# A first MLP layer by seven products in halves of 128 tokens, with its weight factors streamed from device memory

## The chip, the cores and the metric

The kernel runs on one core of one Trainium2 chip. The metric is the device time of one execution in microseconds (us), taken several times; the median counts. Beside the times there is one profiled execution, and all durations below come from it. Engines are named as the profile names them: PE multiplies matrices and PEld loads its stationary operand, DVE and ACT and POOL work on vectors (PSUM, where PE leaves its sums, is read by DVE and ACT alone), and SP is a queue that issues transfers and does nothing else here.

## The reference

Attention with a threshold, and then a two-layer MLP over the same tokens:

```python
q, k, v: (8, 8, 576, 64) float32         # batch, heads, sequence, head dim
scores = (1 / sqrt(64)) * q @ k^T
scores = where(scores >= max(scores) - tau, scores, -1e9)
attn   = softmax(scores) @ v
x      = attn as (8 * 576, 512)           # 4608 tokens, heads side by side
h      = x @ w_in                         # w_in: (512, 2048)
g      = max(h, 0) ** 2
out    = g @ w_out                        # w_out: (2048, 512)
```

Everything is float32. A float32 matmul stands in the profile as two records, each with a weight load of its own.

## The kernel before

All engines run in an order written out by the program: the order in which the Python code issues instructions is the order of each engine's queue, and each queue is strictly in order.

**Attention.** Two heads are a pair; there are 32 pairs (8 batches of 4). A visit goes through the 576 queries of one pair in steps of 128 queries. Loop `for s in range(END + 1)` (L851) takes one step: `scores` (PE, L246, into the two PSUM tiles `s0`, `s1`, then a maximum by DVE, L268), `exponents` (ACT, L281 to L284), `threshold` (DVE, L296), `divide` (POOL, L304 and L306), all on the same step. In the larger part of the run (steps from `first_dma` on) the step's weights are transposed one step later in blocks of 32x32 by DVE (`turn_blocks`, L370, into `turned`), and `place_blocks` moves the blocks into the tile `wT` by transfers of 36 or 72 KB that SP issues (L382, L387), 16 for each two steps. There is one `wT`. At the end of a visit `mix` (PE, L432) multiplies `wT` with the values and ACT copies the result to `xT`, a ring of 5 x 256 tokens.

**MLP.** The 4608 tokens are 18 chunks of 256. When a batch's attention is done, its chunks join the list `waiting` as pieces of about 1.76 us of PE time (`PIECE_US`). `fill` (L769) takes pieces from this list four times a step, so that PE has work while the other engines do attention. A piece returns a function with the work on its result (reading PSUM out, squaring); `after` (L760) issues this function behind the next piece's matmuls, and what that function returns behind the one after.

Chunk 0 is plain in both layers. In chunks 1 to 15 the first layer is plain (`mlp_in`, L473: 16 pieces of 4 matmuls, 128x128 weights against 256 tokens, two pieces to a PSUM bank, then relu on ACT, L492, and the square on POOL, L493). Their second layer is `product` (L540): the seven products of Strassen's scheme in Winograd's form, each 8 matmuls of 128 tokens' sums against 256 columns. `square_half` (POOL, L470, L471) makes two of the sums that it needs. The last two chunks, 16 and 17, share one first layer by seven products in halves of 256 tokens (`pair_in`, L635): its operands' sums are made by DVE (`pair_sums`), `w_in` stays in SBUF, and the seven results are put together by DVE (L659 to L668).

`next_bank` (L315) hands out PSUM banks 4 to 7 in turn; `mix`, `mlp_in` and `product` all take from it.

Of the kernel before, what the change touches and what calls it, by code (L numbers as in the profile page):

```python
# [9 lines left out]
FP32 = mybir.dt.float32  # L10
U32 = mybir.dt.uint32
AF = mybir.ActivationFunctionType
ALU = mybir.AluOpType
# [6 lines left out]
def kernel(  # L20
# [24 lines left out]
    HF, HD = NFT // 2, d_model // 2  # L45
    SCALE = 0.125
# [5 lines left out]
    psum = ctx.enter_context(tc.tile_pool(name="psum", bufs=1, space=bass.MemoryType.PSUM))  # L52

# [4 lines left out]


# [34 lines left out]
    p1s = const.tile([P, HD], FP32, name="p1s")  # L94
    p5s = const.tile([P, HD], FP32, name="p5s")
# [213 lines left out]
    used = {"tx": 0, "mm": 0, "bank": 7}  # L309

# [4 lines left out]
    def next_bank():  # L315

        among = (4, 5, 6, 7) if state["step"] > first_dma + 2 else (6, 7)
        used["bank"] = min([x for x in among if x > used["bank"]] or among)
        return bank[used["bank"]]

# [146 lines left out]
    def square_half(lo, g=g, gsum=gsum):  # L467

        f = slice(lo, lo + HF // 2)
        nc.gpsimd.tensor_tensor(out=gsum[0][:, f, :], in0=g[:, f, P:], in1=g[:, lo + HF:lo + HF + HF // 2, P:], op=ALU.add)  # L470
        nc.gpsimd.tensor_tensor(out=gsum[1][:, f, :], in0=gsum[0][:, f, :], in1=g[:, f, 0:P], op=ALU.subtract)  # L471

    def mlp_in(j, x):  # L473

        f, at = FORDER[x], j * TCH % RING
        if x % 2 == 0:
            used["h"] = take("mm", (6, 7)) if j < PLAIN else next_bank()
# [6 lines left out]
        posts = []  # L484
        if j == PAIR - 1 and x > 1:
            posts.append(lambda: pair_sums(1, PAIR_EARLY))
        if j == PLAIN:
            posts.append(lambda: some_sums(1))
        if x % 2:
            def square():  # L490
                to = g[:, f - 1:f + 1, :]
                nc.scalar.activation(out=to, in_=h, func=AF.Relu)  # L492
                nc.gpsimd.tensor_tensor(out=to, in0=to, in1=to, op=ALU.mult)  # L493
                if j >= PLAIN and x % 8 == 7:
                    square_half(x // 8 * (HF // 2))
            posts.append(square)
        return posts
# [40 lines left out]
    PRODUCTS = ("1", "5", "6", "2", "7", "4", "3")  # L538

    def product(j, x, half):  # L540

        if half == 0:
            used["p"] = next_bank()
        to = used["p"][:, 0:HD]
        p = PRODUCTS[x]
        g, gsum = (g_pair, gsum_pair) if j == PAIR + 1 else squares
# [9 lines left out]
        if j == PAIR - 1:  # L556
            pair_sums(1, 0)
# [7 lines left out]
        def then():  # L565
            add, sub, tt, u = ALU.add, ALU.subtract, nc.vector.tensor_tensor, u_sum
            if p == "1":
# [25 lines left out]
    squares = g, gsum  # L593
    PAIR = NCH - 2
    at0, at1, at2 = (x * TCH % RING for x in (PAIR, PAIR + 1, PAIR + 2))
    assert (at1, at2) == (at0 + TCH, at0 + 2 * TCH) and at2 + 2 * TCH <= RING
    DH = d_ff // 2
    wT_flat = wT.rearrange("p c n -> p (c n)")
    mS1, mS2 = (wT_flat[:, x * 2 * DH:(x + 1) * 2 * DH].rearrange("p (c n) -> p c n", c=2) for x in range(2))
    g_pair = turned[:, 0:NFT * TCH].rearrange("p (f n) -> p f n", f=NFT)  # L600
    flat_slots = [x.rearrange("p u k -> p (u k)") for x in w_slots[0:2]]
    gsum_pair = [x[:, 0:HF * P].rearrange("p (f n) -> p f n", f=HF) for x in flat_slots]
    xS = [flat_slots[x // 2][:, x % 2 * 2 * TCH:(x % 2 + 1) * 2 * TCH].rearrange("p (c n) -> p c n", c=2)
          for x in range(4)]
    x11, x12, x21, x22 = (xT[:, c:c + 2, at:at + TCH] for c in (0, 2) for at in (at0, at1))
    temps = [x[:, 0:2 * TCH] for x in (qT, kT[0], kT[1])] + [wT_flat[:, 4 * DH:4 * DH + 6 * TCH]]
    temps = [x[:, i:i + TCH] for x in temps for i in range(0, x.shape[1], TCH)]
    pair_p1, pair_tmp = temps[0:2], temps[2:]

    def quarter_sums():  # L610

        add, sub = ALU.add, ALU.subtract
        cols = [(c, slice(h * WP, (h + 1) * WP), slice(DH + h * WP, DH + (h + 1) * WP)) for c in range(2) for h in range(2)]
        for c, lo, hi in cols:
            yield mS1[:, c, lo], w_in_sb[:, c, hi], w_in_sb[:, 2 + c, hi], add
        for c, lo, hi in cols:
            yield mS2[:, c, lo], mS1[:, c, lo], w_in_sb[:, c, lo], sub
        yield xS[0], x12, x11, sub
        yield xS[1], x22, xS[0], sub
        yield xS[2], x22, x12, sub  # L620
        yield xS[3], xS[1], x21, sub
        for c, lo, hi in cols:
            yield w_in_sb[:, c, hi], w_in_sb[:, c, lo], w_in_sb[:, c, hi], sub
        for c, lo, hi in cols:
            yield xT[:, 2 * c + lo.start // WP, at2:at2 + WP], w_in_sb[:, 2 + c, lo], mS2[:, c, lo], sub

    quarters = list(quarter_sums())
    PAIR_EARLY = 8

    def pair_sums(count, keep):  # L630
        for to, a, b, op in quarters[:max(min(count, len(quarters) - keep), 0)]:
            nc.vector.tensor_tensor(out=to, in0=a, in1=b, op=op)
            quarters.pop(0)

    def pair_in(j, f):  # L635

        assert not quarters
        lo, hi = slice(f * P, (f + 1) * P), slice(DH + f * P, DH + (f + 1) * P)
        S4 = [xT[:, 2 * c + f // 4, at2 + f % 4 * P:at2 + f % 4 * P + P] for c in range(2)]
        part = {1: ([w_in_sb[:, c, lo] for c in range(2)], x11), 2: ([w_in_sb[:, 2 + c, lo] for c in range(2)], x21),  # L640
                3: (S4, x22), 4: ([w_in_sb[:, 2 + c, hi] for c in range(2)], xS[3]),
                5: ([mS1[:, c, lo] for c in range(2)], xS[0]), 6: ([mS2[:, c, lo] for c in range(2)], xS[1]),
                7: ([w_in_sb[:, c, hi] for c in range(2)], xS[2])}
        if f == 0:
            used["pair"] = [psum.tile([P, 2, 512], FP32, tag=f"s{u}", name=f"pair{u}")[:, 0, :] for u in range(2)]
            used["pair"] += [bank[x] for x in range(4, 8)]
        ps = {}
        for x, what in enumerate(((1, 6), (2, 7), (5, 3), (4,))):
            b = used["pair"][(4 * f + x) % 6].rearrange("p (h n) -> p h n", h=2)
            for y, p in enumerate(what):  # L650
                ps[p] = b[:, y, :]
                for c in range(2):
                    nc.tensor.matmul(ps[p], part[p][0][c], part[p][1][:, c, :], start=(c == 0), stop=(c == 1))  # L653

        def then():
            add, sub, tt = ALU.add, ALU.subtract, nc.vector.tensor_tensor
            p1 = pair_p1[f % 2]
            nc.scalar.copy(p1, ps[1])
            u2, u3, u4, c11, c12, c21, c22 = pair_tmp[0:7]  # L659
            tt(out=u2, in0=ps[6], in1=p1, op=add)  # L660
            tt(out=c11, in0=ps[2], in1=p1, op=add)
            tt(out=u3, in0=ps[7], in1=u2, op=add)
            tt(out=u4, in0=ps[5], in1=u2, op=add)
            tt(out=c22, in0=ps[5], in1=u3, op=add)
            tt(out=c12, in0=ps[3], in1=u4, op=add)
            tt(out=c21, in0=u3, in1=ps[4], op=sub)
            for to, c in ((g[:, f, :], c11), (g[:, HF + f, :], c21), (g_pair[:, f, :], c12), (g_pair[:, HF + f, :], c22)):
                nc.vector.scalar_tensor_tensor(out=to, in0=c, scalar=0.0, in1=c, op0=ALU.max, op1=ALU.mult)  # L668
            if f % 4 == 3:
                square_half(f - 3)  # L670
            if f == HF - 1:
                for x in (0, HF // 2):
                    square_half(x, g_pair, gsum_pair)
        return [then]

# [13 lines left out]
    PLAIN = 1  # L691
# [38 lines left out]
    def pieces_of(j):  # L730

        todo = [((x // 4 + 1) * NMC, mlp_in, j, x) for x in range(NFT)]
        if j >= PAIR:
            todo = [(n_pieces, pair_in, j, f) for f in range(HF)] if j == PAIR else []
        if j < PLAIN:
            todo += [(n_in + min(f + 1 + f // (NFT - 2), NFT), mlp_out, j, f) for f in range(NFT)]
        else:
            todo += [(n_pieces, product, j, x, half) for x in range(len(PRODUCTS)) for half in range(2)]
        return todo

    def add_chunk(j):
        waiting.extend(pieces_of(j))

# [25 lines left out]
    def fill(us):  # L769
        state["left"] += us  # L770
        while waiting and state["left"] >= PIECE_US / 2 and waiting[0][0] <= state["usable"]:
            _, fn, *what = waiting.popleft()
            state["left"] -= PIECE_US
            if fn in (mlp_out, pair_in) or what[0] in (*range(PLAIN + 1), PAIR) and what[1] == 0:
                after()
# [18 lines left out]
    def end_rounding(p):  # L794
        round_weights(p, 4)
        state["rounded"] += 1
        if p + RAW < n_pieces:
            load_weights(p + RAW)
# [182 lines left out]
```

## Time and profile before

| | |
|---|---|
| median of 3 runs | 1380.3 us (1380.26 to 1381.9) |
| the profiled execution's span | 1377.9 us, 2.4 us under the median |
| PE busy | 1345.0 us, 98% of the span |
| DVE, ACT, POOL busy | 874.8, 433.3, 880.8 us |
| first layer, chunks 0 to 15 (L480) | 2048 matmul records |
| first layer, chunks 16 and 17 (L653) | 224 matmul records |
| SP: transfers into `wT` (L382, L387) | 992 |
| POOL: transfers of q, k, v (L190) | 416 |

A record's duration runs from its start to the last result written, and the next record starts before that; so spacing between starts, not duration, is what a record costs PE. The table of engines therefore does not tell how close PE is to its limit; the chain of waits and the timeline do.

### The profile page before, as it was taken

The numbers are of one execution on the slowest core, as the hardware profiler recorded it, in microseconds if no ns is written. First come the engines' busy times: TensorE is split into PE (matmuls) and PEld (weight loads), VectorE is DVE, ScalarE is ACT, GpSimd is POOL, SyncE is SP. The second block draws the span as 40 slices with busy tenths as digits, with TensorE's granted clock in tenths as the row PEclk, the third lists the DMA queues.
The fourth block names the chain that finished last, engine by engine and source line by source line (L and its number), as shares of the span: only waits on it lengthen the run. The fifth ranks groups of instructions, "written<-read, shape, count | busy, mean of one in ns | idle before, by whom it ended". The sixth has DMA issues, their size and how long they took to land.

```text
span 1377.9 us, 22712 instructions
## 1 busy us (share of the span) xinstructions
PE 1345.0 (98%) x7544; PEld 1031.9 (75%) x7544; DVE 874.8 (63%) x1974; ACT 433.3 (31%) x1060; POOL 880.8 (64%) x1193
## 2 busy tenths in 40 slices
PE   6898999999999999999999999999999999999998
PEld 5676557777777777777777777777777777788887
DVE  6877675967767676757575666566666666432551
ACT  4777674223232323232322222222222232200000
POOL 3678874768786868676767768585868665513121
PEclk8999999999999999999999999999999999999999
DMA  8764530445646455554445455545445544320000
GB/s 154 161 153 112 148 87 25 91 84 106 118 95 116 98 107 118 103 114 86 96 84 114 87 112 107 105 74 105 89 104 98 118 82 94 64 56 0 16 0 31
DMA packets 407875, 127.94 MB, mean 93 GB/s; under 512 B 390832, under 2 KB 396752, under 8 KB 407760
## 3 DMA queue, kind: packets, MB, share of 16 engines
q1 hardware_dynamic: 385632, 95.10, 36.6%
q0 software_dynamic: 19824, 31.11, 8.4%
q8 instruction: 61, 1.00, 0.3%
q10 hardware_dynamic: 2304, 0.29, 0.2%
q14 instruction: 54, 0.44, 0.1%
HBM read 50.59 MB, written 9.44 MB: 44 GB/s over the span
## 4 chain that ended last, share of the span: by engine, by line
PE 89%; ACT 3%; DVE 3%; POOL 2%; issue 1%; DMA 1%; SPq 0%; ACTq 0%; DVEq 0%; POOLq 0%
PE bank L480 31%; PE bank L555 29%; PE s L246 12%; PE bank L432 11%; PE bank L653 2%; PE bank L521 2%; PE bank L330 2%; PE pair L653 1%; ACT wT L331 1%; ACT w L284 1%; DVE wo L509 1%; DVE w L296 1%; DVE st L268 1%; POOL g L493 0%; POOL w L306 0%
## 5 line engine op out<-in xcount | busy, mean ns | idle before, releaser
L480 PE MATMUL bank<-xT,w_in_sb 128*128 128x256 f32 x2048 | 464.8, 383 | 3.1 <-POOL w_in_sb L147 2.1
L480 PEld LDWEIGHTS bank<-xT,w_in_sb 128*128 128x128 f32 x2048 | 382.1, 190 | 79.2 <-issue 21.7
L268 DVE TENSOR_REDUCE st<-s 128x1 f32<-128x576 f32 x286 | 204.1, 752 | 220.8 <-PE s L246 220.8
L296 DVE SCALAR_TENSOR_TENSOR w<-s,st,w 128x576 f32<-128x576 f32 x269 | 209.3, 815 | 120.5 <-ACT w L284 120.4
L306 POOL TENSOR_SCALAR w<-w,st 128x576 f32<-128x576 f32 x269 | 222.7, 837 | 25.4 <-DVE st L299 19.6
L555 PE MATMUL bank<-wo,gsum 128*128 128x256 f32 x1024 | 234.6, 382 | 2.3 <-POOL gsum L470 2.3
L555 PEld LDWEIGHTS bank<-wo,gsum 128*128 128x128 f32 x1024 | 191.8, 190 | 39.8 <-issue 9.8
L281 ACT ACTIVATE st<-st 128x2 f32<-128x2 f32 (+1 forms) x148 | 30.3, 205 | 564.9 <-DVE st L268 564.3
L284 ACT ACTIVATE w<-s,st 128x576 f32<-128x576 f32 x269 | 183.4, 732 | 0.2 <-ACT st L282 0.2
L370 DVE STREAM_TRANSPOSE turned<-w 128x512 f32<-128x512 f32 (+2 forms) x388 | 168.8, 489 | 20.0 <-DMA wT<-turned 17.9
L555 PE MATMUL bank<-wo,g 128*128 128x256 f32 x768 | 177.5, 382 | 0.0
L246 PE MATMUL s<-kT,qT 64*128 64x288 f32 x1016 | 165.8, 431 | 11.9 <-DVE w L296 8.0
L493 POOL TENSOR_TENSOR g<-g 128x512 f32<-128x512 f32 x128 | 135.7, 1061 | 62.4 <-ACT g L492 61.0
L304 POOL TENSOR_SCALAR st<-st 128x2 f32<-128x2 f32 (+1 forms) x148 | 32.7, 221 | 221.0 <-DVE w L296 214.9
L432 PE MATMUL bank<-wT,vs 128*64 128x128 f32 (+7 forms) x1700 | 167.8, 356 | 5.0 <-ACT wT L331 3.5
L555 PEld LDWEIGHTS bank<-wo,g 128*128 128x128 f32 x768 | 143.9, 190 | 28.7 <-issue 8.7
L432 PEld LDWEIGHTS bank<-wT,vs 128*64 128x64 f32 (+1 forms) x1700 | 95.6, 136 | 76.8 <-issue 24.3
L246 PEld LDWEIGHTS s<-kT,qT 64*128 64x128 f32 x1016 | 94.4, 187 | 68.2 <-issue 47.7
L492 ACT ACTIVATE g<-bank 128x512 f32<-128x512 f32 x128 | 76.5, 600 | 114.2 <-PE bank L480 113.6
L190 POOL DMA_DIRECT2D vs<-in_v_dram x144 | 90.5, 634 | 0.0
L470 POOL TENSOR_TENSOR gsum<-g 128x512 f32<-128x512 f32 x32 | 41.4, 1293 | 48.0 <-DVE g L668 45.7
L145 POOL TENSOR_TENSOR turned<-turned 128x512 f32<-128x512 f32 x32 | 41.0, 1286 | 40.4 <-DVE turned L143 34.5
(130 smaller groups left out, 1185.2 us busy)
## 6 DMA issues: line engine op xcount, KB each, us to landing
wT<-turned SPq DMA_DIRECT2D x800, 72.0 KB, 2.3
wo<-in_moe_w_in_dram SPq DMA_DIRECT2D x16, 512.0 KB, 4.7
wo<-in_moe_w_out_dram SPq DMA_DIRECT2D x16, 512.0 KB, 3.6
out_dram<-osb POOLq DMA_DIRECT2D x32, 256.0 KB, 2.9
ql<-in_q_dram POOLq DMA_DIRECT2D x96, 72.0 KB, 2.7
wT<-turned SPq DMA_DIRECT2D x192, 36.0 KB, 2.3
kl<-in_k_dram POOLq DMA_DIRECT2D x88, 72.0 KB, 3.0
vs<-in_v_dram POOLq DMA_DIRECT2D x48, 128.0 KB, 3.2
```

Source lines behind the costliest of these rows:

```text
L190: (nc.gpsimd if state["step"] > first_dma + 2 else nc.sync).dma_start(out=to, in_=src)
L246: nc.tensor.matmul(sc[u][to, half, 0:HALF], lhsT, keys[rows, half * HALF:(half + 1) * HALF], start=True, stop=True)
L268: nc.vector.tensor_reduce(out=mx[:, u:u + 1], in_=sc[u][:, :, 0:HALF], axis=AX.XY, op=ALU.max)
L284: nc.scalar.activation(out=w[:, u, :].rearrange("p (h k) -> p h k", h=2), in_=sc[u][:, :, 0:HALF], func=AF.Exp, bias=bias[:, u:u + 1], sca ...
L296: nc.vector.scalar_tensor_tensor(out=wu, in0=sc[u][:, :, 0:HALF], scalar=thr[:, u:u + 1], in1=wu, op0=ALU.is_ge, op1=ALU.mult, accum_out=s ...
L306: nc.gpsimd.tensor_scalar(out=w[:, u, :], in0=w[:, u, :], scalar1=z[:, u:u + 1], scalar2=rcp[:, u:u + 1], op0=ALU.add, op1=ALU.mult)
L370: nc.vector.transpose(wb[:, at:at + k1 - k0, i % 2, :], w[:, u, k0 * 32:k1 * 32].rearrange("p (k q) -> p k q", q=32))
L432: nc.tensor.matmul(ps[u * D:(u + 1) * D, :], vs[n % 2][rows, u * (NBLK + 1) + c, :], wT[rows, NBLK if c == NBLK else u * (NBLK + 1) + c, a ...
L480: nc.tensor.matmul(h[:, x % 2, :], w_in_sb[:, c, f * P:(f + 1) * P], xT[:, c, at:at + TCH], start=(c == 0), stop=(c == NMC - 1))
L492: nc.scalar.activation(out=to, in_=h, func=AF.Relu)
L493: nc.gpsimd.tensor_tensor(out=to, in0=to, in1=to, op=ALU.mult)
L555: nc.tensor.matmul(to, left[:, f, :], wo[:, slot, f, :], start=(f == 0), stop=(f == HF - 1))
```

## The change

From chunk 1 on, each chunk has a first layer of its own by seven products (Winograd's form again), in halves of 128 tokens, 256 model columns and 1024 hidden columns. It is done in 14 pieces, `unit`: seven products for each half `q` of the hidden columns' quarters (4 blocks of 128). A unit has 8 matmuls of 128x128 weights against 128 tokens. The two-chunk version (`pair_in`) goes, and the plain version stays for chunk 0 alone (`PLAIN = 1` in both kernels).

The products' sums are chained in PSUM: products 1, 6, 7 and 4 add up in one bank, and after each the bank is read out before the next may add to it; 5 and 3 share a second bank, 2 has a third. The order is 1, 2, 6, 5, 7, 3, 4. `keep_bank` withholds a bank from `next_bank` while its chain is open.

The seven factors of `w_in` (four are sums, `factor_sums`, eight DVE operations of 1024 elements) are written to device memory during the early steps, 14 blocks of 512 KB. `w_in_sb` then becomes seven slots of 512 KB. A unit's block is fetched into its slot by `load_unit`, on SP's queue: when unit `u` of the first seven has been used, its slot gets unit `u + 7` of the same chunk; after the second seven, unit `u - 7` of the next chunk. The load is issued with the function that reads the unit's result, so behind the next unit's matmuls, and in SP's queue it stands where the code then is, among the transfers of `place_blocks`.

In the main loop one more `after()` stands behind `scores`. The product order of the second layer becomes 1, 2, 5, 6, 7, 4, 3. Units wait until every weight is rounded and step `first_dma + 2` is past, where the plain first layer of chunk 1 began earlier.

```diff
+    factors = dram.tile([2 * NU, P, DH], FP32, name="factors")
+    slots = [flat_in[:, x * DH:(x + 1) * DH].rearrange("p (c f) -> p c f", c=2) for x in range(NU)]
...
+    def load_unit(j, u):
+        nc.sync.dma_start(out=slots[u % NU].rearrange("p c f -> p (c f)"), in_=factors[u])
...
+    def token_sums(j):
...
+        for to, a, b in ((xS[0], x12, x11), (xS[1], x22, xS[0]), (xS[2], x22, x12), (xS[3], x21, xS[1])):
+            nc.vector.tensor_tensor(out=to, in0=a, in1=b, op=ALU.subtract)
...
+    def unit(j, u):
+        q, p = u // NU, UNITS[u % NU]
...
+        if p in "125":
+            used[p] = keep_bank((q, p))
+        to = used[{"6": "1", "7": "1", "4": "1", "3": "5"}.get(p, p)].rearrange("p (f n) -> p f n", f=4)
+        left = slots[u % NU]
+        for f in range(4):
+            for c in range(2):
+                nc.tensor.matmul(to[:, f, :], left[:, c, f * P:(f + 1) * P], part[:, c, :],
+                                 start=(p in "125" and f == 0 and c == 0), stop=(p in "234" and f == 3 and c == 1),
+                                 skip_group_check=True)
...
+        def square(to, src=None):
+            nc.scalar.activation(out=to, in_=to if src is None else src, func=AF.Relu)
+            nc.gpsimd.tensor_tensor(out=to, in0=to, in1=to, op=ALU.mult)
+        def then():
+            more = []
+            if p == "1":
+                nc.scalar.copy(g11, to)
+            elif p == "2":
+                nc.vector.tensor_tensor(out=g11, in0=to, in1=g11, op=ALU.add)
+                del kept[q, "2"]
+                more = [lambda: square(g11)]
+            elif p == "6":
+                nc.scalar.copy(g12, to)
+            elif p == "5":
+                nc.scalar.copy(p5, to)
+            elif p == "7":
+                nc.scalar.copy(g22, to)
+                nc.gpsimd.tensor_tensor(out=g22, in0=g22, in1=p5, op=ALU.add)
+            elif p == "3":
+                nc.vector.tensor_tensor(out=g12, in0=to, in1=g12, op=ALU.add)
+                del kept[q, "5"]
+                more = [lambda: square(g12)]
+            else:
+                square(g21, to)
+                del kept[q, "1"]
+                square(g22)
+                more = [lambda: square_half(4 * q)]
+            if u + NU < 2 * NU:
+                load_unit(j, u + NU)
+            elif j + 1 < NCH:
+                load_unit(j + 1, u - NU)
+            return more
+        return [then]
...
-    PRODUCTS = ("1", "5", "6", "2", "7", "4", "3")
+    PRODUCTS = ("1", "2", "5", "6", "7", "4", "3")
...
-    def pair_in(j, f):
...
-        todo = [((x // 4 + 1) * NMC, mlp_in, j, x) for x in range(NFT)]
-        if j >= PAIR:
-            todo = [(n_pieces, pair_in, j, f) for f in range(HF)] if j == PAIR else []
         if j < PLAIN:
+            todo = [((x // 4 + 1) * NMC, mlp_in, j, x) for x in range(NFT)]
...
-            todo += [(n_pieces, product, j, x, half) for x in range(len(PRODUCTS)) for half in range(2)]
+            todo = [(n_pieces + 1, unit, j, u) for u in range(2 * NU)]
+            todo += [(n_pieces + 1, product, j, x, half) for x in range(len(PRODUCTS)) for half in range(2)]
...
+        if p + 1 in (n_in // 2, n_in):
+            adds, stores = factor_sums((p + 1) // (n_in // 2) - 1)
+            early_work.extend((adds[x] if x < 4 else []) + (stores[x - 1] if x else []) for x in range(5))
...
+        if s == first_dma:
+            assert read_to["x"] == PLAIN * TCH and not early_work
+            for u in range(NU):
+                load_unit(PLAIN, u)
...
             if s != 1:
                 scores(s)
+                after()
```

## The prediction

> **What bounds the kernel now.** I read the table of engines first, then the chain of waits, then the groups by line.
>
> ```profile
> PE 1345.0 (98%) x7544; PEld 1031.9 (75%) x7544; DVE 874.8 (63%) x1974; ACT 433.3 (31%) x1060; POOL 880.8 (64%) x1193
> PE 89%; ACT 3%; DVE 3%; POOL 2%; issue 1%; DMA 1%; SPq 0%; ACTq 0%; DVEq 0%; POOLq 0%
> L480 PE MATMUL bank<-xT,w_in_sb 128*128 128x256 f32 x2048 | 464.8, 383 | 3.1 <-POOL w_in_sb L147 2.1
> ```
>
> The chain runs through PE for 89% of the span, and the 2048 first-layer records wait 3.1 us in all. The chain's end shows matmuls back to back:
>
> ```profile
> 1225.61 27.82 PE bank L480 x128
> 1253.43 24.17 PE bank L555 x112
> ...
> 1325.95 48.36 PE bank L555 x224
> ```
>
> 24.17 / 112 is 0.216 us a record of 256 columns. So PE streaming is the bound, and every gap that PE gets is paid. In the attention part a step looks like this (timeline of PE, then of SP over the same stretch):
>
> ```profile
> 452.27 7.17 PE L480 MATMUL bank<-xT,w_in_sb 128*128 128x256 f32 x32
> 459.38 1.24 PE L246 MATMUL s<-kT,qT 64*128 64x288 f32 x8
> 460.55 7.17 PE L480 MATMUL bank<-xT,w_in_sb 128*128 128x256 f32 x32
> ```
> ```profile
> 441.00 5.76 SPq L387 DMA_DIRECT2D wT<-turned  x8
> 446.86 23.88 SPq L382 DMA_DIRECT2D wT<-turned  x32
> ```
>
> Scores take 1.17 us, four pieces 7.1 us. SP is no engine of the first table, but its queue is full for long stretches: 40 transfers in 30 us, at 0.675 us each where none waits (612 ns in the median, and the gap behind it). Once a visit it also waits, for the blocks that DVE turns (SP's waits):
>
> ```profile
> SPq L382 <- DVE turned L370: 111.6, 27, 8.3
> ```
>
> **The change part by part.** *PE, removed.* 15 chunks x 128 records x 0.216 = 414.7 us, and the two-chunk first layer, from 1277.61 to 1325.95 in the chain: 48.4. Together 463.1 us.
>
> *PE, added.* 17 chunks x 14 units x 8 matmuls x 2 = 3808 records of 128 columns and 128 tokens. No such record is in the trace; these bound it:
>
> ```profile
> 182.46 0.82 PE L330 MATMUL bank<-ident,w 128*128 128x128 f32 x6
> ```
> ```profile
> 140.14 0.55 PEld L432 LDWEIGHTS bank<-wT,vs 128*64 128x64 f32 x16 [0.33 <-issue]
> ```
> ```profile
> 452.27 0.30 PEld L480 LDWEIGHTS bank<-xT,w_in_sb 128*128 128x128 f32 x2 [0.39 <-issue]
> ```
>
> Six transposes of 128 columns: (0.82 - 0.27) / 5 = 0.109 us apart (one lasts 273 ns); that is the lower end. Two weight loads of 190 ns are done in 0.30 us, so a load holds its place for 0.11 us, no longer than 128 tokens stream (half of 0.216). Where load and stream are equally short (64 columns, 64 tokens; eight pairs, side by side in two column groups), pairs follow at (0.55 - 0.14) / 7 = 0.059 us, against 0.054 of streaming: the tie costs 5 ns. The upper end is a load that hides nothing of its 190 ns. I take 0.1115, by the tie: 424.6 us, so PE saves 38.5 us; at 0.109 it saves 48, at 0.1135 it saves 31, at 0.190 it loses 260.
>
> Here the Trainium skill speaks against the change: "TensorE: Matmul & The Clock Gate", section "The mechanism", has weight loads overlap running matmuls only in another row group. By it a record would cost load plus stream, an estimated 0.213 us, and the first layer some 350 us more. The row against it: at 256 columns records follow at 0.216 us, each with a 190 ns load.
>
> *The loads.* 238 loads of 512 KB come into SP's queue. The nearest row is the weights' (512 KB, L125), 328 to 587 ns to issue, and:
>
> ```profile
> DMA to landing us min/median/max: 3.3/4.4/6.5
> ```
>
> A unit of the second seven waits for a load that is issued after the unit seven before it is done, and behind what SP holds then. I laid SP's queue in the new program's order beside PE's, with 0.675 us for a transfer into `wT`, 0.45 for a load, 4.4 to land, 1.17 for scores, 1.78 for a unit, and transposes done 6.8 us after their step's scores, as here, where scores end at 452.3:
>
> ```profile
> 457.56 1.51 DVE L370 STREAM_TRANSPOSE turned<-w 128x512 f32<-128x512 f32 x4
> ```
>
> Chunk 3 worked out, from the end E of the scores before its first unit: 16 transfers in front of its loads wait for that step's transposes, E + 6.8. They take 10.8, so the first load is issued at E + 17.6 and lands at E + 22. PE does three units (5.3), scores, four units (7.1), scores, and wants unit 7 at E + 14.8: 7.2 us late. The following loads come in a row and keep pace. Laid out so for all chunks, 15 loads in 12 of them are late by 0.7 to 9.3 us, 94 us in all; 11 are over 5. The chunks behind the attention have no transfers in the way: none late. Laid out the same way, the old program's SP issue times follow the trace within some 2%, the trace being slower by PE's small gaps; these give each load about 0.7 us, so I take 84 us. Landing at 3.3 or 6.5 makes it 68 or 120.
>
> Late `wT` transfers in turn would hold `mix` (its last one was issued near 470.7, it began at 477.1). In the new order long rows of loads stand where SP waits for `mix` anyway: nothing, but 1 us a visit, 28 us, if not.
>
> *The clock.* PE has no pause of several us after the start. There it has one of 3.91 us, ending at 14.97:
>
> ```profile
> 6.40:13.20 6.80, 3.05 (x23) 2.17 (x21) 4.66 (x8) 1.73 (x6) 0.00 (x0) 1.00 0.69 118
> 13.20:20.00 6.80, 5.03 (x17) 3.69 (x17) 6.52 (x17) 3.70 (x10) 3.69 (x6) 0.50 0.88 263
> ```
>
> The third figure from the end is the granted clock: 0.50 until 20.0, for 5 us after PE resumed, 2.5 us lost. 14 of the late loads stop PE for 3.7 us or more; at 1.5 us each I add 20, between nothing and 35.
>
> *Reading out.* A unit's bank must be read within one unit's time (1.78). After scores, ACT waits for DVE's maxima and does two exponentials; it is free 3.2 us after scores end (447.2 against 444.0) and then copies for 0.6 us (L492's 600 ns): 0.25 us late for the third unit, 0.95 where a relu stands ahead. By the queue order 13 steps have the longer form (nine of them unit "6" behind "2") and 13 the shorter: 16 us together, over half of it where a late load is waited for anyway. I take 5 (0 to 16). POOL gets two more adds a chunk (1.29 us each) beside squares and `divide`, near full in these steps: 3 (0 to 15), as product "5" now comes third, behind 6.9 us of products.
>
> *DVE and the start.* Eight adds of 1024 elements, 1.4 to 2.0 us each by rows of 512 (687, 1021 ns), fall where DVE is 70% busy: 4 (0 to 16). Two steps lose their filler before `first_dma + 2`, some 1.5 us each: 3. Token sums, the new PSUM adds and the DVE work of the removed version lie beside PE; if DVE were late, SP's wait for its transposes would grow by as much. The tail has 1.78 us a unit and a copy of 0.6 + 0.2: nothing.
>
> *Sum.* 1377.9 - 38.5 + 84 + 20 + 5 + 3 + 4 + 3 = 1458.4; with the 2.4 us between span and median 1461 us.
>
> **The rivals.** *A, the other side: loads in time.* If SP got to the loads at once, as a queue with gaps would, they would land 4.4 us after a unit, with 10.7 us to spare, and no clock would be lost: 1380.3 - 38.5 + 15 = 1357, faster. For it: the chain has 1% of DMA and 0% of SP, and the transfer engines are busy for 0.51 of the time from 250 to 1200 us. Against it: the 32 transfers in 23.88 us that nothing can pass. It decides below 23 us of waits and lost clock, 1.6 us a late load. The skill's "DMA: Bandwidth & Descriptors", section "Issuing engines are not separate DMA queues", calls issue time usually small beside the transfer; by it this rival would hold. Here a transfer into `wT` takes 0.675 us of SP's time and lands in 2.3.
>
> *B: the weight load sets the pace of short matmuls.* At 0.190 us a unit lasts 3.0 us, so PE wants unit 7 at E + 23.6 and the loads are in time: 1380.3 + 260 + 15 = 1655. Against it: the tie at 64 columns.
>
> *C: the change doesn't do what it says.* The second layer and attention are the same count of records; nothing speaks for it.
>
> **How the numbers follow.** Late loads 0.84, A 0.11, B 0.04, small mixtures 0.01. The first case gives 1461; its ends are 1400 (landing 3.3, no clock loss, saving 48) and 1510 (6.5, full clock loss), since the bounds will not all fall together. 1400 to 1510 holds 0.80. Faster by over 0.2% (2.8 us, about what a measurement tells from no change) 0.10, within it 0.02, slower 0.88.
>
> **What would show it.** Right: units of 16 records in 1.78 us; PE idle before certain units with the releaser "DMA w_in_sb<-factors", 3.5 to 9 us each, about one a chunk up to the end of attention; granted clock below 1.00 behind them; loads issued in rows behind 16 `wT` transfers. Wrong: units at 3 us (B), idle time of units put down to ACT rather than DMA, or loads that SP issues within some 5 us of the unit.

## The result and the profile after

The changed kernel takes 1504.0 us (median of 4 runs, 1498.7 to 1507.7) against 1380.4: a ratio of 1.089 (95% interval 1.086 to 1.092), so 9% slower. Forecast were 1461 us, 1400 to 1510. The profiled execution took 1507.5 us, its span 1505.8. One execution of e4 below took 1759.6 us at a mean granted clock of 0.75, in a slower state that no other execution here shows; it is left out of e4's time.

The page after, in the order of the lines shown of before (engine table, granted clock, chain of waits, first-layer groups, loads):

```profile
PE 1359.9 (90%) x9208; PEld 1100.0 (73%) x9208; DVE 903.5 (60%) x2010; ACT 513.9 (34%) x1204; POOL 949.6 (63%) x1243
...
PEclk8999998898989899998999999999999999999999
...
PE 67%; SPq 8%; DMA 8%; DVE 7%; ACT 4%; issue 3%; POOL 2%; ACTq 0%; DVEq 0%; POOLq 0%
...
L561 PE MATMUL bank<-w_in_sb 128*128 128x128 f32 x2176 | 270.2, 282 | 32.6 <-DMA w_in_sb<-factors 28.8
...
L561 PE MATMUL bank<-xT,w_in_sb 128*128 128x128 f32 x1632 | 221.1, 297 | 62.8 <-DMA w_in_sb<-factors 52.9
...
w_in_sb<-factors SPq DMA_DIRECT2D x238, 512.0 KB, 5.6
wT<-turned SPq DMA_DIRECT2D x800, 72.0 KB, 2.7
```

PE falls from 98% of the span to 90%, and from 89% of the chain to 67%. What came in is SP's queue (0 to 8%) and DMA (1 to 8%). The first layer, which waited 3.1 us before, has 95.4 us of idle time in front of its two groups of records, 81.7 of it for loads (83.1 in the sum below, where a wait begins when the last record's columns have streamed, not when its last result is written). The clock row has an 8 in seven slices; before it had one:

```profile
PEclk8999999999999999999999999999999999999999
```

PE's waits after, with the total, the times and the longest:

```profile
PE bank L561 <- DMA w_in_sb<-factors: 81.7, 18, 10.0
PE s L254 <- DVE w L304: 15.2, 10, 3.9
PE bank L561 <- DVE g L589: 7.2, 2, 3.6
PE bank L661 <- DVE gsum L676: 4.4, 2, 2.3
...
PE bank L661 <- DVE g L589: 3.9, 2, 3.7
```

In the chain's end, behind the attention part, first and second layers alternate (L561 has 128 columns, L661 256):

```profile
1403.59 25.01 PE bank L561 x224
1428.60 24.18 PE bank L661 x112
```

25.01 / 224 is 111.7 ns a record: the first layer itself is faster, 25.0 us for 256 tokens where it was 27.8.

Where the time went can be summed from PE's records alone. From the start of one record to the start of the next, time up to the full-speed streaming of its columns counts as streaming; what a stretch at half clock adds counts as lost clock; the rest is idle time, put down to what released the next record. "Early" is the first 250 us. These figures, here and in the table of experiments, are worked out from the records; no view prints them.

| us | before | after | difference | forecast |
|---|---|---|---|---|
| streaming | 1261.1 | 1224.8 | -36.3 | -38.5 |
| waits for factor loads | 0 | 83.1 | +83.1 | +84 |
| `mix` waiting for `wT` | 0 | 1.0 | +1.0 | 0 |
| lost clock | 3.5 | 43.9 | +40.4 | +20 |
| other idle, early | 52.6 | 60.2 | +7.6 | +7 (adds 4, filler 3) |
| other idle, later | 52.6 | 83.3 | +30.7 | +8 (reading out 5, POOL 3) |

The differences sum to 126.5 of the span's 127.9.

Chunk 3, which the prediction worked by hand, on PE and then on SP:

```profile
404.05 1.24 PE L254 MATMUL s<-kT,qT 64*128 64x288 f32 x8
405.22 3.84 PE L561 MATMUL bank<-xT,w_in_sb 128*128 128x128 f32 x32
...
419.92 1.24 PE L254 MATMUL s<-kT,qT 64*128 64x288 f32 x8
428.08 6.60 PE L561 MATMUL bank<-xT,w_in_sb 128*128 128x128 f32 x32 [6.92 <-DMA w_in_sb<-factors]
```
```profile
400.34 23.53 SPq L398 DMA_DIRECT2D wT<-turned  x32
423.97 14.64 SPq L530 DMA_DIRECT2D w_in_sb<-factors  x11
```

E is 405.2. SP issues the first load at E + 18.8 (forecast 17.6), behind 32 transfers in 23.5 us; the second 16 of these begin at E + 6.9, with that step's transposes (6.8). PE wants unit 7 at E + 15.9 (14.8) and starts it at E + 22.9 (22): 6.9 us late against 7.2. The clock behind it, over three stretches (third figure from the end):

```profile
421.00:428.00 7.00, 0.16 (x2) 0.00 (x0) 5.00 (x12) 2.80 (x6) 6.83 (x8) 0.69 0.89 220
428.00:431.40 3.40, 3.32 (x15) 3.32 (x16) 0.00 (x0) 0.00 (x0) 3.21 (x6) 0.50 1.01 412
431.40:434.80 3.40, 3.40 (x22) 3.40 (x21) 0.01 (x1) 0.59 (x1) 0.35 (x1) 0.63 1.04 415
```

After the pause PE runs at half speed for 3.4 us and a good part of the next 3.4. One pause of 6.9 us costs some 3 us more in this way (0.50 of 3.4 and 0.37 of 3.4).

### The profile page after: what moved, and what is told of

It reads as the page before. It is cut to its first block, busy times and chain, and to the rows that moved or that the text cites. A ratio compares the mean times of both kernels' runs of the same rounds, so it can differ in the third digit from the quotient of the medians.

```text
span 1505.8 us, 26813 instructions
## 1 busy us (share of the span) xinstructions
PE 1359.9 (90%) x9208; PEld 1100.0 (73%) x9208; DVE 903.5 (60%) x2010; ACT 513.9 (34%) x1204; POOL 949.6 (63%) x1243
## 4 chain that ended last, share of the span: by engine, by line
PE 67%; SPq 8%; DMA 8%; DVE 7%; ACT 4%; issue 3%; POOL 2%; ACTq 0%; DVEq 0%; POOLq 0%
PE bank L661 23%; PE bank L561 22%; PE s L254 10%; PE bank L448 9%; SPq L398 7%; DMA w_in_sb<-factors 5%; DVE st L276 2%; DMA wT<-turned 2%; PE bank L626 2%; ACT w L292 2%; DVE w L304 1%; PE bank L346 1%; DVE turned L386 1%; ACT wT L347 1%; PE bank L496 1%
## 5 line engine op out<-in xcount | busy, mean ns | idle before, releaser
L561 PE MATMUL bank<-w_in_sb 128*128 128x128 f32 x2176 | 270.2, 282 | 32.6 <-DMA w_in_sb<-factors 28.8
L561 PEld LDWEIGHTS bank<-w_in_sb 128*128 128x128 f32 x2176 | 256.6, 196 | 50.3 <-issue 33.4
L561 PE MATMUL bank<-xT,w_in_sb 128*128 128x128 f32 x1632 | 221.1, 297 | 62.8 <-DMA w_in_sb<-factors 52.9
L304 DVE SCALAR_TENSOR_TENSOR w<-s,st,w 128x576 f32<-128x576 f32 x269 | 209.2, 815 | 106.5 <-ACT w L292 106.4
L561 PEld LDWEIGHTS bank<-xT,w_in_sb 128*128 128x128 f32 x1632 | 210.8, 210 | 76.2 <-DMA w_in_sb<-factors 33.1
L661 PE MATMUL bank<-wo,gsum 128*128 128x256 f32 x1088 | 249.6, 384 | 4.4 <-DVE gsum L676 4.4
L661 PEld LDWEIGHTS bank<-wo,gsum 128*128 128x128 f32 x1088 | 204.9, 191 | 44.8 <-issue 15.5
L661 PE MATMUL bank<-wo,g 128*128 128x256 f32 x816 | 188.1, 384 | 6.8 <-DVE g L589 3.9
L254 PE MATMUL s<-kT,qT 64*128 64x288 f32 x1016 | 174.4, 442 | 19.1 <-DVE w L304 13.0
L661 PEld LDWEIGHTS bank<-wo,g 128*128 128x128 f32 x816 | 153.1, 191 | 37.3 <-issue 10.6
L386 DVE STREAM_TRANSPOSE turned<-w 128x512 f32<-128x512 f32 (+2 forms) x388 | 169.0, 490 | 14.8 <-DMA wT<-turned 10.8
L570 ACT ACTIVATE g<-g 128x512 f32<-128x512 f32 x102 | 62.2, 627 | 40.5 <-DVE g L589 14.4
```

The source lines that it names most:

```text
L254: nc.tensor.matmul(sc[u][to, half, 0:HALF], lhsT, keys[rows, half * HALF:(half + 1) * HALF], start=True, stop=True)
L304: nc.vector.scalar_tensor_tensor(out=wu, in0=sc[u][:, :, 0:HALF], scalar=thr[:, u:u + 1], in1=wu, op0=ALU.is_ge, op1=ALU.mult, accum_out=s ...
L386: nc.vector.transpose(wb[:, at:at + k1 - k0, i % 2, :], w[:, u, k0 * 32:k1 * 32].rearrange("p (k q) -> p k q", q=32))
L561: nc.tensor.matmul(to[:, f, :], left[:, c, f * P:(f + 1) * P], part[:, c, :], start=(p in "125" and f == 0 and c == 0), stop=(p in "234" a ...
L661: nc.tensor.matmul(to, left[:, f, :], wo[:, slot, f, :], start=(f == 0), stop=(f == HF - 1))
```

## The experiments

Theory: the loads are late by their place in SP's queue, and each wait also costs clock. Rival 1: the transfers are too slow. Rival 2: reading out the chained bank is the cost. The columns below are those of the sum above.

| kernel | us | ratio to before, 95% | load waits | `wT` waits | lost clock | other idle, later |
|---|---|---|---|---|---|---|
| changed kernel | 1504.0 | 1.089 (1.086 to 1.092) | 83.1 | 1.0 | 43.9 | 83.3 |
| e1 loads on POOL | 1523.6 | 1.105 (1.102 to 1.109) | 16.6 | 60.7 | 42.6 | 100.0 |
| e2 no later loads | 1397.5 | 1.012 (1.010 to 1.014) | 0 | 0.1 | 16.3 | 84.4 |
| e3 quarter loads, SP | 1467.2 | 1.063 (1.060 to 1.066) | 52.4 | 0.3 | 35.1 | 82.3 |
| e4 PE busy in eight waits | 1493.3 | 1.081 (1.078 to 1.084) | 49.3 | 0.5 | 26.2 | 84.1 |
| e5 quarter loads, POOL | 1433.9 | 1.039 (1.037 to 1.041) | 0.1 | 0.2 | 26.5 | 109.3 |
| e6 on POOL, half of them later | 1512.3 | 1.095 (1.090 to 1.099) | 16.1 | 63.6 | 39.1 | 96.8 |
| e7 no later loads, oldest bank | 1377.6 | 0.9984 (0.9975 to 0.9994) | 0 | 0.1 | 8.5 | 71.0 |
| e8 all loads, oldest bank | 1497.3 | 1.085 (1.083 to 1.086) | 89.6 | 1.1 | 38.5 | 72.2 |
| e9 half the loads, SP | 1500.0 | 1.085 (1.082 to 1.088) | 93.7 | 0.1 | 41.9 | 70.9 |
| e10 half the loads, POOL | 1450.7 | 1.050 (1.045 to 1.056) | 19.5 | 27.2 | 24.6 | 80.9 |
| e11 half the loads, SP, first | 1460.7 | 1.057 (1.055 to 1.059) | 63.3 | 0.6 | 32.8 | 69.1 |

The early idle time is 58.6 to 62.7 in all of them. e4's last four figures are from its second execution with a profile (1496.3 us).

### e1: the loads on another queue

```diff
-        nc.sync.dma_start(out=slots[u % NU].rearrange("p c f -> p (c f)"), in_=factors[u])
+        nc.gpsimd.dma_start(out=slots[u % NU].rearrange("p c f -> p (c f)"), in_=factors[u])
```

> Edit: the 238 factor loads are issued from POOL's queue instead of SP's; the bytes and the order of PE are the same. Theory (the loads are late because they stand behind the transfers into wT in SP's queue): PE's waits for factor loads, 83 us in the changed kernel, fall under 15 us, the clock loss behind them (44 us) under 20, and the time to 1390 to 1430 us, the upper part if POOL's 238 issues of some 0.6 us (150 us) hold its squares. Rival 1 (the transfers themselves or the device memory are too slow for 122 MB): the waits stay over 50 us and the time over 1460. Rival 2 (reading out the chained bank is what costs): the waits for loads go, but come back as waits for ACT, DVE and POOL, and the time stays over 1470.

1523.6 us, slower still: above the 1390 to 1430 of the theory, and not for the reason that either rival gave. The waits for loads did go, from 83.1 to 16.6 us (under 15 expected); in their place PE waits for the transfers into `wT`. PE's waits of e1:

```profile
PE bank L448 <- DMA wT<-turned: 60.9, 9, 15.4
PE s L254 <- DVE w L304: 19.1, 13, 3.9
PE bank L561 <- DMA w_in_sb<-factors: 14.2, 12, 2.7
```

The stretch in front of the longest of these waits, which begins at 342 (last two figures: busy share of the 16 transfer engines, GB/s):

```profile
325.00:335.00 10.00, 9.58 (x81) 8.77 (x80) 6.08 (x14) 3.72 (x8) 9.79 (x17) 1.00 0.96 236
335.00:345.00 10.00, 6.97 (x56) 5.62 (x54) 7.69 (x19) 5.30 (x12) 9.75 (x13) 1.00 1.11 227
```

Loads and transfers into `wT` now run side by side, the engines are full (0.96 and 1.11; the share adds up the packets' times and can pass 1), and both take longer: 6.9 us a load in the median (5.6 in the changed kernel), 4.0 a transfer of 72 KB into `wT` (2.7), at most 20.6 (9.2). So the place in SP's queue did make the loads late, but it had also kept the two kinds of transfers from meeting. The Trainium skill, "DMA: Bandwidth & Descriptors", section "Issuing engines are not separate DMA queues", says that transfers from all engines run on the same 16 DMA engines and interleave; these rows agree. The same section calls issue time usually small beside the transfer. Here one transfer into `wT` takes some 0.67 us of SP's time and lands in 2.7, but the issues add up in one queue: in chunk 3, 32 of them held SP for 23.5 us.

### e2: no loads after the first seven

```diff
-            if u + NU < 2 * NU:
-                load_unit(j, u + NU)
-            elif j + 1 < NCH:
-                load_unit(j + 1, u - NU)
```

> Edit: after the first seven loads no factor is loaded again; every unit multiplies with what is in its slot. The loads after the first seven are left out. Theory (waits for loads and the half clock behind them are 110 to 125 us of the changed kernel's 1504): 1380 to 1400 us, clock loss under 15 us, and some 30 to 40 us more PE idle time than in the kernel before, which are waits for the bank, for DVE and POOL. Rival 2 (reading out the chained bank costs it): over 1440. If the prediction's 8 us for reading out and POOL had been right: 1360 to 1368.

1397.5 us, as expected; the clock loss, 16.3 us, is a little over the 15 expected. The loads thus cost 106.5 us, of which 83.1 are their waits and 27.6 clock (43.9 less 16.3), less some 3 us of other idle time. What stays is a surprise for the prediction's rival A, which had put a kernel with loads in time at 1357: free loads alone do not make the change pay.

### e3: a quarter of the bytes, at the same place

```diff
-        nc.sync.dma_start(out=slots[u % NU].rearrange("p c f -> p (c f)"), in_=factors[u])
+        part = DH if j == PLAIN and u < NU else DH // 4
+        nc.sync.dma_start(out=slots[u % NU].rearrange("p c f -> p (c f)")[:, 0:part], in_=factors[u][:, 0:part])
```

> Edit: every load after the first seven brings only a quarter of the factor (128 KB), at the same place in SP's queue. Three quarters of each factor are left out. Theory (place in the queue): only the landing gets shorter, 5.6 to about 2.5 us; by the queue laid out for the prediction the waits for loads change by some 14 us for each us of landing, so 35 to 60 us of 83 remain, and the time is 1440 to 1480. Rival 1 (bytes): waits under 15 us and a time under 1410.

PE's longest item of waits in e3, and its row of issues (KB each, us to landing):

```profile
PE bank L562 <- DMA w_in_sb<-factors: 51.1, 11, 6.4
```
```profile
w_in_sb<-factors SPq DMA_DIRECT2D x231, 128.0 KB, 2.7
```

Three quarters fewer bytes leave 52.4 of 83.1 us of waits. Over all loads the median landing is 2.9 us shorter, so 10.6 us of waits per us of landing (14 expected). But the loads that PE waits for (18 in the changed kernel, 11 here) stand first in their row, directly behind a transfer into `wT`, in 16 of the 18 and in all 11 cases; they landed in 4.3 and 2.7 us in the median, and by these it is some 18 us of waits per us. Place, not size, makes most of the lateness on SP.

### e4: PE kept busy in eight waits

```diff
+    BUSY = {(1, 8): 2, (2, 7): 7, (3, 7): 6, (4, 8): 9, (5, 10): 9, (6, 7): 5, (9, 7): 4, (13, 7): 4}
...
+        for x in range(BUSY.get((j, u), 0)):
+            nc.tensor.matmul(to.rearrange("p f n -> p (f n)"), wo[:, Q00, 7, 0:P],
+                             wo[:, Q00, 0:2, :].rearrange("p a d -> p (a d)"), start=True, stop=True)
```

> Edit: in front of eight units whose load was late (54 us less 4 of waits in all) PE does 46 idle matmuls of 512 columns (0.855 us each at full clock, 39 us in all) into the bank that the unit then overwrites; nothing else waits for them. Theory (the granted clock falls because PE stood still): the half-clock stretches behind these eight waits go, 15 to 25 us of the 44, and the time falls to 1480 to 1492 though PE does more work. Rival (the clock loss has another cause, or work in the waits delays the units): 1500 to 1515.

1493.3 us: faster by 11 us with 39 us more of work on PE, just short of the 1480 to 1492 expected. The same kernel once more, for its profile:

> The kernel with idle matmuls in eight waits once more, for its profile (1493 us before). Theory (PE standing still lowers the clock): the half-clock stretches behind these eight waits are gone, and the clock loss is 25 to 32 us instead of 44. Rival: it stays over 38 us, and the 11 us came from elsewhere.

Chunk 3 in it, on PE, and the clock after the wait:

```profile
415.83 5.42 PE L562 MATMUL bank<-wo 128*128 128x512 f32 x12
423.17 3.84 PE L566 MATMUL bank<-xT,w_in_sb 128*128 128x128 f32 x32 [1.93 <-DMA w_in_sb<-factors]
426.84 3.74 PE L566 MATMUL bank<-w_in_sb 128*128 128x128 f32 x32
```
```profile
424.00:431.00 7.00, 7.00 (x63) 6.83 (x64) 0.69 (x1) 2.08 (x4) 3.43 (x5) 1.00 1.04 376
```

The unit waits for its load as before, but PE stands still for 1.9 us instead of 6.9, the clock is 1.00 behind it, and two units take 3.8 us instead of 6.6. The lost clock falls from 43.9 to 26.2 us, as expected. That PE's pauses cost clock is shown.

### e5: quarter loads on POOL

The edits of e1 and e3 together.

> Edit: the loads come from POOL's queue and, after the first seven, bring only a quarter of a factor. Three quarters of each factor are left out. New theory, after the loads on POOL's queue gave 1523.6 us with 60.5 us of waits of `mix` for wT: the place in SP's queue made the loads late, and once it is gone the loads and the transfers into wT share the 16 transfer engines, which were at 0.94 to 1.11 of their time in those stretches. Then a quarter of the bytes on POOL leaves neither wait: under 10 us for loads, under 10 us for wT, 1395 to 1415 us (1397.5 without loads). Rival (POOL's issuing, 130 us, or the order on POOL delays the transposes that wT waits for): wT waits stay over 40 us and the time over 1450.

```profile
PE s L254 <- DVE w L304: 20.1, 14, 3.9
PE bank L662 <- POOL g L572: 15.8, 7, 4.3
```
```profile
L531 POOL DMA_DIRECT2D w_in_sb<-factors x238 | 135.5, 570 | 21.8 <-PE bank L562 21.8
```

Both kinds of waits are gone, as the theory of shared engines has it; 1433.9 us is between the two forecasts. The 36 us above e2 (1397.5) lie elsewhere: POOL is busy for 135.5 us with issuing, its squares come later (PE waits 15.8 us for them, 2.9 in the changed kernel), the other idle time rises by 25 us and the lost clock by 10. These 36 us go with the loads on POOL; no run has POOL's issues without the transfers, so that the issues alone cost them is not shown. Another queue is not free either.

### e6: half of the loads later

```diff
         if not half:
+            if j + 1 < NCH:
+                load_unit(j + 1, x)
             return []
```

and the loads for the next chunk go from the units; on POOL's queue as in e1.

> Edit: whole loads from POOL's queue, but the seven for the next chunk go out one per product instead of one per unit of the second seven. Theory (bursts: while 14 units run, 14 loads of some 1.85 us of all engines meet the transfers into wT): `mix` waits for wT 20 to 40 us instead of 60, the time 1440 to 1490. Rival (the mean use of the transfer engines, 0.82 from 250 to 1260 us, decides, whenever the loads are issued): 1505 to 1530.

1512.3 us with 63.6 us of waits for `wT`, as its rival had it. The theory of bursts falls in this form: moving seven of fourteen loads into the products leaves the sum of the waits for `wT` as it was. That these loads now collide beside the products instead, where transfers into `wT` run too, is the likely reason; it was not looked at load by load. Mean use of the transfer engines from 250 to 1260 us is 0.82 in e1 and in e6.

### e7 and e8: which bank is taken next

```diff
-        used["bank"] = min([x for x in among if x > used["bank"]] or among)
+        used["bank"] = min(among, key=lambda x: taken.index(x))
+        taken.remove(used["bank"])
+        taken.append(used["bank"])
```

and a kept bank goes to the end of `taken` when it is let go. What it is about, in the changed kernel, DVE and then PE:

```profile
758.40 0.81 DVE L304 SCALAR_TENSOR_TENSOR w<-s,st,w 128x576 f32<-128x576 f32 x1
...
760.34 1.51 DVE L386 STREAM_TRANSPOSE turned<-w 128x512 f32<-128x512 f32 x4
761.77 0.65 DVE L589 TENSOR_TENSOR g<-bank,g 128x512 f32<-128x512 f32 x1
```
```profile
756.93 1.95 PE L561 MATMUL bank<-w_in_sb 128*128 128x128 f32 x16
762.48 6.66 PE L561 MATMUL bank<-xT,w_in_sb 128*128 128x128 f32 x32 [3.60 <-DVE g L589]
```

Unit "3" is done near 757; the add that reads its bank stands in DVE's queue behind a step's threshold and transposes until 761.8, and the next unit has been given this very bank. e7 has the edit without later loads, e8 with all of them.

> Edit, on the kernel without later loads (1397.5 us): a new bank is the one that has been free longest, instead of the next by number. The loads after the first seven are left out. Theory (some 20 of the 42 us that PE idles more than in the kernel before are waits for a bank whose reader stands late in DVE's or ACT's queue, with another bank long free): 1375 to 1388 us, and the waits for DVE's adds out of the bank, 12 us, go. Rival (the readers are late for every bank, or DVE is late with the sums themselves): 1393 to 1400.

> Edit: the changed kernel with all its loads, a new bank being the one that has been free longest. Theory (the waits for a bank add to the waits for loads): 15 to 24 us less than the changed kernel's 1504, as without loads (1397.5 to 1377.6): 1480 to 1489. Rival (a unit that waits less for its bank waits longer for its load): 1497 to 1506.

Without loads: 1377.6 us, 20 less, as expected; the waits for L589 are gone (11.3 us in e2), other idle time falls by 13.4 and lost clock by 7.8. With loads it is only 7 us, as the rival had it (1497 to 1506): the waits for loads rise by 6.5, since a unit that is not held by its bank comes sooner to a load that is still on its way. Both causes are real, and they overlap. e7 is also the nearest to a bound for this change that was measured: with the later loads left out and the best choice of bank found, it is 0.2% faster than the kernel before.

### e9 and e10: half as many loads

```diff
-        q, p = u // NU, UNITS[u % NU]
+        q, p = (u // NU + j - PLAIN) % 2, UNITS[u % NU]
...
-            elif j + 1 < NCH:
-                load_unit(j + 1, u - NU)
```

The loads take the same `q`, the products take the feature halves in the chunk's order, and the bank is the oldest. The first seven units of a chunk find their factors in the slots. e9 loads from SP's queue, e10 from POOL's.

> Edit: oldest bank as before, and every second chunk takes the two halves of the features in the other order, so that its first seven units use what the chunk before left in the slots: 119 loads instead of 238, all of them for second sevens, at the same place in SP's queue. Theory (place: the 18 late loads are all of second sevens, and stand behind the same transfers): waits for loads 55 to 80 us, time 1445 to 1480. Rival (bytes): waits under 30 us and a time under 1420.

> Edit: the same 119 loads from POOL's queue. Theory (transfer engines: their mean use from 250 to 1260 us falls from 0.82 to about 0.66): `mix` waits for wT 10 to 35 us where it waited 60 to 64, POOL's issuing costs half of the 36 us that the quarter loads on POOL cost: 1395 to 1440. Rival (the use within the first seven units' 14 us decides, 7 loads of 1.85 us there as before, or the waits for wT have another cause): waits over 50 us, 1450 to 1490.

The waits of PE for loads in e9 (SP):

```profile
PE bank L570 <- DMA w_in_sb<-factors: 92.3, 15, 10.4
```

and its waits for both kinds of transfer in e10 (POOL):

```profile
PE bank L457 <- DMA wT<-turned: 26.9, 4, 13.5
...
PE bank L570 <- DMA w_in_sb<-factors: 15.7, 15, 4.3
```

On SP, half the bytes change nothing: 1500.0 us beside e8's 1497.3, 93.7 us of waits beside 89.6. The waits are above the forecast range (55 to 80 us), and so is the time (1445 to 1480), but the rival, bytes, is out by far (under 30 us, under 1420). On POOL, where the place is not the limit, the same halving takes the time from 1523.6 to 1450.7 and the waits for `wT` from 60.7 to 27.2, at a mean use of the transfer engines of 0.68 instead of 0.82; part of these 73 us is the oldest bank's (at most the 20 of e7), and some may be the halved issuing's on POOL. The cleaner pair is e1 and e5, both on POOL with 238 loads and the same choice of bank: a quarter of the bytes takes 1523.6 to 1433.9 us and the waits for `wT` from 60.7 to 0.2. There the bytes decide, as the theory of shared engines says. e10's time is above its 1395 to 1440, and its waits for `wT` are within their 10 to 35.

### e11: another order in SP's queue

```diff
-        for what in place_at[s]:
+        late = any(x[1] is unit and x[3] < NU for x in list(waiting)[:8])
+        for what in [] if late else place_at[s]:
             place_blocks(*what)
...
+        for what in place_at[s] if late else []:
+            place_blocks(*what)
```

the second pair of lines behind the step's last filler.

> Edit, on the kernel with 119 loads on SP's queue (1500.0 us, 93.7 us of waits for loads): in steps with units of a first seven, the step's transfers into wT are put behind the step's loads instead of in front of them; mostly that lets one to six loads pass in front of 16 transfers. The bytes are the same. Theory (place): the first load behind the 16 transfers is then issued some 10.8 us after its slot came free and lands 5.5 later, against 14.9 us until PE wants it, so about 2 to 4 us late instead of 7: waits for loads 30 to 55 us, waits of `mix` for wT under 20, time 1445 to 1475. Rival (the queue only changes hands: wT is as late as the loads were): waits for wT over 30 us, time over 1485.

SP around chunk 3 in e11, and PE's waits for loads:

```profile
395.40 1.02 SPq L539 DMA_DIRECT2D w_in_sb<-factors  x2
397.74 12.04 SPq L407 DMA_DIRECT2D wT<-turned  x16
409.88 2.76 SPq L539 DMA_DIRECT2D w_in_sb<-factors  x5
```
```profile
PE bank L570 <- DMA w_in_sb<-factors: 61.9, 14, 8.6
```

Against e9 only the order in the queue differs: 39 us faster, waits for loads 63.3 instead of 93.7, waits for `wT` 0.6. Two loads pass in front of 16 transfers, and the third is now the late one: PE waits 3.3 us for it at 413.9, where it waits 6.8 us in this chunk in e9. The time is inside the forecast range, the waits are above theirs (30 to 55), so the estimate of 2 to 4 us a late load was too low (61.9 us in 14 waits, 4.4 in the mean). That the place in the queue makes the waits is shown by this run best of all: same bytes, same queue, same PE order.

No complete version came near the kernel before; the best is e10, 5% slower.

## Why the prediction was right

The direction, the mechanism and its place held; the middle was 43 us low, by two terms.

- *PE streaming.* 111.7 ns a record where 111.5 was taken, between bounds of 109 and 113.5; the saving is 36.3 us, forecast 38.5. Rival B (weight loads set the pace, 1655) is out. The Trainium skill's rule in "TensorE: Matmul & The Clock Gate", section "The mechanism", which would have had load and stream add up to an estimated 0.213 us, does not fit this case: each of these records has a weight load of 196 to 210 ns on average beside it.
- *The loads.* 84 us forecast, 83.1 measured, in 18 waits; chunk 3 came within 1.2 us at each of its points. The landing of 4.4 us, taken from the weights, held for the 18 loads that PE waited for (4.3 in the median; all 238: 5.6). That the total came so close is partly luck: 15 late loads were forecast, 11 of them over 5 us, and 18 came, 8 of them over 5. The cause that was named, the place behind `wT` transfers, is shown by e11 and e9, and e3 shows the part of the landing.
- *`mix`.* Nothing forecast, 1.0 us measured. The reason given, that SP waits for `mix` anyway, is not tested by itself; the transfers into `wT` had slack as long as the loads stood in the same queue, and had none in e1.
- *The clock.* The term was mis-sized: 20 us forecast (0 to 35), 40.4 measured. Two things were too low. The loads' own share was 27.6 (e2): 14 pauses of 3.7 us or more at 1.5 us each were forecast, and 11 of that length came, so each cost more, up to some 2.5 us (the 7 shorter waits may have a part); chunk 3's cost 3. And the pauses that are not loads were left out: without any later load 12.8 us more clock is lost than before, and 7.8 of that goes with the bank waits (e7).
- *Reading out and POOL.* The term was mis-sized: 8 us forecast, 30.7 measured. I had looked at ACT and POOL behind a unit, and put "the new PSUM adds" of DVE beside PE. Some 11 us of PE's waits were for one of these adds (7.3 and 4.2 us of idle time in front of first and second layer), and 4.7 for `gsum`. The step that failed is "lie beside PE": an add that a bank waits for is on the path when a threshold and four transposes stand in front of it and the next unit has been given that bank. With the oldest bank these waits are gone and 13.4 of the 31.8 us are back (e2 and e7); what the rest consists of is known only in part.
- *Early.* 7 forecast, 7.6 measured; whether adds and lost filler share it as forecast was not tested.
- *Rival A.* Its 1357 us was too low by 20 to 40: e2 has 1397.5 and e7 1377.6. It took the clock and the reading out as vanishing with the waits. (Its "10.7 us to spare" is the whole time of the six units in between; a landing of 4.4 leaves 6.3.) And its condition, "if SP got to the loads at once", does not lead there: off SP's queue the loads meet the transfers into `wT` on the same engines. "Transfer engines are busy for 0.51 of the time" was read as room; with the loads the mean is 0.77 to 0.82, and a stretch where both run is full.
- *The range.* Its low end does not follow from the three bounds beside it: landing, clock and saving take 16, 20 and 9.5 us off 1461, which gives 1415, not 1400. The measured time is near the other end, 6 us inside it.

## What to carry to other kernels

When a change streams operands that were resident, lay out the issuing queue in program order and ask for each load what stands in front of it; then ask what the two kinds of transfer do to each other if they run at once, because the queue that delays one of them may be what keeps the other in time. Price each new pause of a busy PE twice, for the pause and for the half clock behind it. Where banks are chained over several matmul groups, the reader's place in its own engine's queue decides when the bank comes free, so take the bank that has been free longest.

## What the runs showed that was not expected

- Taking the loads off the crowded queue made the kernel slower (1523.6 against 1504.0 us).
- Halving the bytes changed nothing on one queue (1500.0 against 1497.3) and went with 73 us on the other, at most 20 of them by the other choice of bank.
- The first layer's seven products are worth 36 us of streaming and, with free loads and the better bank choice, 2.6 us of time: 8.5 us more of other idle time early, 18.4 later and 5.0 of clock take back 31.9 (e7 against before).
- A bank chosen by number instead of by age cost 20 us where nothing else hid it, and 7 where late loads did.
- 238 issues of 570 ns on POOL went with 36 us of time (e5 against e2), though POOL was busy for only 68% of the span without them.
